# Packed attention and a channel mixer on one core: the value loads by every second partition instead of by head

## The chip, the cores and the metric

The kernel runs on one core of a Trainium2 chip. The metric is the device time of one launch in microseconds (us). A profiled execution also gives a span, the time from the first to the last instruction, and the launch takes a little longer than that. Engines are named as the profile names them: PE (TensorE, the matrix engine), DVE (VectorE), ACT (ScalarE), POOL (GpSimd) and SP (SyncE, which here only issues transfers). A transfer is issued by one instruction of SP and is then carried out by the core's 16 DMA engines.

## The reference

There are 8 batches and 8 heads of 64 elements, with 576 tokens. Each head has 32 pack queries `p`. Everything is float32, except that the mixer's weights are float64 and arrive as pairs of 32-bit words.

```python
scale = 1.0 / np.sqrt(q.shape[-1])
def sm_attn(qq, kk, vv):
    s = scale * np.matmul(qq, kk.transpose(0, 1, 3, 2))
    s = s - np.max(s, axis=-1, keepdims=True)
    a = np.exp(s)
    a = a / (np.sum(a, axis=-1, keepdims=True) + 1e-09)
    return np.matmul(a, vv)
p_packed = sm_attn(p, k, v)          # 32 packed rows per head
attn = sm_attn(q, p_packed, p_packed)
x = attn.transpose(0, 2, 1, 3).reshape(B, S, H * D)
h = x.transpose(0, 2, 1) @ U @ V     # mixing over the 576 tokens, rank 32
u = x + h.transpose(0, 2, 1)
out = u + np.maximum(u @ w_ch1, 0.0) @ w_ch2   # 512 -> 2048 -> 512
```

## The kernel before

**Two stages.** The first stage computes the packed rows `p_packed` of all batches. Its unit of work is one batch and one group `g` of four heads, so there are 16 units (`UN`, line 386). The second stage runs over the 8 batches and does the attention of `q` to the packed rows, the mixing, and the two large matrix products; these are written in three-product form to keep float32 accuracy (`mm3`, line 84).

**The first stage, lines 485 to 536.** In iteration `i` of the loop over units the program turns back the exponentials of unit `i-1`, computes the scores of unit `i`, loads the values of unit `i+1` (`a_load_v`, line 403), transposes the keys of unit `i+1` (`a_turn`), loads the keys of unit `i+2` (`a_load`; with them, once per batch, the pack queries `pn`), and takes the softmax of unit `i`. Then it converts one chunk of the float64 weight `w1` (`some_w1`; the chunk comes by line 137 into a tile `bits`, ACT takes its absolute value at line 143, DVE does lines 78 to 81). After that it multiplies unit `i-2`'s exponentials by its values (`a_pack`, PE line 467, ACT line 469) and transposes the packed rows of unit `i-3` (`a_heads`, ACT line 478). After each second unit `a_heads` writes the tile `ppTa` to device memory by line 483; that tile has one buffer, so the next copy of line 478 waits until the store has been read out. Iterations 4 and later also carry three steps each of the second stage's attention for batch 0 (its queries come by line 206). Iteration 14 starts on the second weight (`load_w2`, line 151; conversion lines 77 to 81 and 158).

**The values.** Token `n` of 576 is written as `n = 9*i + c`, with 64 rows `i` and 9 columns `c`. A unit's values sit in the tile `vt` of 128 partitions by 5 by 256 elements, with three buffers. Columns 0 to 7 of row `i` lie in partitions `2*i` (columns 0 to 3) and `2*i+1` (columns 4 to 7): each head has four columns of 64 elements, 1 KB, in each partition. Column 8 of all heads lies in `vt[:64, 4]` and comes by a transfer of its own (line 410). In `a_pack` every head's part of `vt` is the moving operand of 4 x 4 matmuls of line 467, and line 410's part that of four more; `a_pack` is the only reader.

**What sets the order.** Up to line 547 the order of instructions on every engine, SP included, is set by a planner that simulates the program as it is emitted (`schedule_with_timeline_sim=True`, line 746): it can place an instruction before or after others that the source lists in another order, and it decides which SP position each transfer gets. From line 548 on (`tc.manual_schedule()`) the order is that of the source. SP is one queue: an issue that has to wait holds up all those behind it. All transfers of this kernel go through it.

Of the kernel before, what the change touches and what calls it, by code (L numbers as in the profile page):

```python
# [19 lines left out]
def packed_attention_mixer_kernel(  # L20
# [27 lines left out]
    nc = tc.nc  # L48
    B, H, S, D = q.shape
# [6 lines left out]
    NT = 9  # L56
# [346 lines left out]
    def a_load_v(u):  # L403
        b, g = UN[u]
        vt = ua[u]["v"] = sT.tile([P, 5, 4 * D], F32, name="vt", bufs=3)
        rows = v[b, 4 * g:4 * g + 4].rearrange("h (i c) d -> i c h d", c=NT)
        main = v[b, 4 * g:4 * g + 4].rearrange("h (i c) d -> h i (c d)", c=NT)[:, :, :8 * D]
        for h in range(4):
            nc.sync.dma_start(out=vt[:, h], in_=main[h].rearrange("i (a x) -> i a x", a=2))
        nc.sync.dma_start(out=vt[:64, 4].rearrange("p (h d) -> p h d", h=4), in_=rows[:, 8])  # L410

    def a_p(b):
# [72 lines left out]
    a_load(0)  # L485
    a_load(1)
    a_load_v(0)
    for n in range(4):
        load_w1(n)
# [12 lines left out]
    for i in range(NU):  # L502
# [3 lines left out]
        if i + 1 < NU:  # L506
            a_load_v(i + 1)
            a_turn(i + 1)
# [242 lines left out]
```

## Time and profile before

Three runs took 861.79, 865.04 and 865.39 us; the median is 865.04 us. The profiled execution:

| what | value |
|---|---|
| the profiled execution's own time | 864.15 us |
| its span | 862.1 us |
| PE busy | 822.1 us, 95% of the span |
| DVE busy | 386.2 us, 45% |
| ACT busy | 326.9 us, 38% |
| transfers of `vt` by line 409 | 64 of 128 KB |
| transfers of `vt` by line 410 | 16 of 64 KB |
| last `vt` issue of line 410 | at 119.1 us |

The page gives busy shares for the whole span, but the two stages have different limits, so it is read by stage. Its strips cut the span into 40 slices of 21.6 us; a digit is the busy share in tenths. The chain of waits follows the work that ended last backwards, from each instruction to what released it; an entry such as "DMA bits" spans from a transfer's issue to its landing, and "SPq L409" is time in which the issue of line 409 itself stood in the way. In the timeline a row gives start, length, engine, line, tiles, and in brackets how long the engine was idle before it and what ended that.

### The profile page before, as it was taken

How to read it: one execution, taken by the hardware profiler on the slowest of the kernel's cores; microseconds unless marked ns; L12 is line 12 of the kernel's file. 1: busy time of each engine (PE TensorE's matmuls, PEld its weight loads, DVE VectorE, ACT ScalarE, POOL GpSimd, SP SyncE). 2: the span in 40 equal slices, each digit the busy share in tenths (PEclk: the TensorE clock that was granted, in tenths of full speed). 3: DMA queues.
4: the chain of work that ended last, by engine and by line, in shares of the span. 5: the costliest groups of instructions: out<-in, count | busy, mean ns of one | idle time of the engine just before them, and what ended most of it. 6: DMA issues, size and time to landing. Idle time of an engine off the chain costs nothing.

```text
span 862.1 us, 14613 instructions
## 1 busy us (share of the span) xinstructions
PE 822.1 (95%) x5792; PEld 658.5 (76%) x5792; DVE 386.2 (45%) x935; ACT 326.9 (38%) x1012; POOL 78.5 (9%) x113
## 2 busy tenths in 40 slices
PE   5878779999999999999999999999999999999997
PEld 3545457778888888887878878888888887888886
DVE  5769756896334423433343433334334234342221
ACT  4547655554333432234233332334233332342221
POOL 0002210111010101110111000110011001000000
PEclk9969899999999999999999999999999999999999
DMA  8999942322100110011001100011001100010001
GB/s 282 278 309 305 297 129 81 105 98 86 50 2 3 59 62 1 1 62 49 1 1 62 49 13 1 1 62 50 1 1 62 61 2 1 1 49 1 1 1 61
DMA packets 38979, 59.08 MB, mean 69 GB/s; under 512 B 11776, under 2 KB 21888, under 8 KB 38912
## 3 DMA queue, kind: packets, MB, share of 16 engines
q1 hardware_dynamic: 38912, 58.16, 20.8%
q8 instruction: 45, 0.74, 0.4%
q14 instruction: 22, 0.18, 0.1%
HBM read 47.79 MB, written 10.35 MB: 67 GB/s over the span
## 4 chain that ended last, share of the span: by engine, by line
PE 81%; DMA 7%; DVE 7%; ACT 2%; SPq 2%; issue 1%; POOL 0%; ACTq 0%; POOLq 0%
PE o L86 16%; PE o L88 16%; PE o L87 16%; PE h_ps L86 8%; PE h_ps L88 7%; PE h_ps L87 7%; DMA bits<-in_moe_w_ch_dram 4%; PE t_ps L367 3%; PE t_ps L239 2%; DMA vt<-in_v_dram 2%; PE t_ps L219 1%; DVE os L80 1%; DMA ppTd<-ppTa 1%; PE t_ps L315 1%; DVE os L79 1%
## 5 line engine op out<-in xcount | busy, mean ns | idle before, releaser
L86 PE MATMUL o<-w2h,hh 128*128 128x512 f32 x512 | 207.2, 405 | 0.0
L88 PE MATMUL o<-w2h,hl 128*128 128x512 f32 x512 | 202.8, 396 | 0.0
L87 PE MATMUL o<-w2l,hh 128*128 128x512 f32 x512 | 202.6, 396 | 0.0
L603 DVE SCALAR_TENSOR_TENSOR hl<-h_ps,hh 128x256 fp32r<-128x256 f32 x256 | 103.8, 422 | 204.0 <-ACT hj L602 192.0
L600 ACT ACTIVATE hh<-h_ps 128x256 fp32r<-128x256 f32 x256 | 98.8, 388 | 186.4 <-PE h_ps L88 185.9
L86 PE MATMUL h_ps<-ah,wth 128*128 128x320 f32 (+1 forms) x512 | 157.5, 308 | 2.1 <-DVE hl L603 2.1
L87 PE MATMUL h_ps<-al,wth 128*128 128x320 f32 (+1 forms) x512 | 151.9, 297 | 0.0
L88 PE MATMUL h_ps<-ah,wtl 128*128 128x320 f32 (+1 forms) x512 | 151.8, 296 | 0.0
L86 PEld LDWEIGHTS h_ps<-ah,wth 128*128 128x128 f32 x512 | 97.0, 189 | 33.6 <-issue 25.2
L88 PEld LDWEIGHTS o<-w2h,hl 128*128 128x128 f32 x512 | 96.7, 189 | 23.0
L86 PEld LDWEIGHTS o<-w2h,hh 128*128 128x128 f32 x512 | 97.1, 190 | 21.5 <-issue 4.6
L87 PEld LDWEIGHTS o<-w2l,hh 128*128 128x128 f32 x512 | 97.1, 190 | 16.8
L87 PEld LDWEIGHTS h_ps<-al,wth 128*128 128x128 f32 x512 | 97.2, 190 | 1.9
L88 PEld LDWEIGHTS h_ps<-ah,wtl 128*128 128x128 f32 x512 | 97.3, 190 | 0.0
L374 DVE TENSOR_TENSOR wtl<-t_ps,wth 128x256 fp32r<-128x256 f32 x128 | 48.5, 419 | 93.0 <-ACT wth L373 89.7
L373 ACT CAST wth<-t_ps 128x256 fp32r<-128x256 f32 x128 | 43.3, 374 | 109.9 <-PE t_ps L367 96.5
L330 POOL TENSOR_TENSOR al<-aT,ah 128x320 fp32r<-128x320 f32 (+1 forms) x32 | 26.0, 813 | 210.5 <-ACT ah L329 210.5
L278 POOL TENSOR_TENSOR e<-e,m 128x576 f32<-128x576 f32 x16 | 18.9, 1181 | 257.5 <-DVE m L277 252.7
L367 PE MATMUL t_ps<-w1t,ppT 64*32 64x512 f32 x512 | 36.0, 601 | 0.5 <-ACT ppTa L478 0.5
L226 ACT COPY xT<-t_ps 128x256 f32<-128x256 f32 x60 | 20.3, 392 | 42.1 <-PE t_ps L219 41.3
L329 ACT CAST ah<-aT 128x320 fp32r<-128x320 f32 (+1 forms) x32 | 13.9, 434 | 44.5 <-DVE aT L328 44.5
L219 PE MATMUL k_ps<-ident,kx 128*128 128x128 f32 x128 | 25.3, 344 | 5.6 <-DMA kx<-in_k_dram 2.9
(130 smaller groups left out, 962.3 us busy)
## 6 DMA issues: line engine op xcount, KB each, us to landing
bits<-in_moe_w_ch_dram SPq DMA_DIRECT2D x32, 512.0 KB, 5.4
kx<-in_k_dram SPq DMA_DIRECT2D x16, 576.0 KB, 5.8
x<-in_q_dram SPq DMA_DIRECT2D x16, 576.0 KB, 4.8
vt<-in_v_dram SPq DMA_DIRECT2D x64, 128.0 KB, 4.9
out_dram<-bits SPq DMA_DIRECT2D x32, 256.0 KB, 2.4
pn<-in_p_dram SPq DMA_DIRECT2D x16, 64.0 KB, 5.0
vt<-in_v_dram SPq DMA_DIRECT2D x16, 64.0 KB, 4.5
out_dram<-os SPq DMA_DIRECT2D x8, 128.0 KB, 2.3
```

The costliest lines, as they stand in the source:

```text
L86: nc.tensor.matmul(ps, lhsT=lh, rhs=rh, start=start, stop=False)
L87: nc.tensor.matmul(ps, lhsT=lh, rhs=rl, start=False, stop=False)
L88: nc.tensor.matmul(ps, lhsT=ll, rhs=rh, start=False, stop=stop)
L219: nc.tensor.transpose(t_ps[:, o:o + P], x[:, h, P * j:P * j + P], ident)
L226: nc.scalar.copy(dst, src[:, a])
L278: nc.gpsimd.tensor_tensor(e, e, m.unsqueeze(2).to_broadcast([P, S // 32, 32]), op=ALU.subtract)
L330: nc.gpsimd.tensor_tensor(al[:, g, ns], aT[:, ns], ah[:, g, ns].bitcast(F32), op=ALU.subtract)
L367: nc.tensor.matmul(f_ps[g][xs], lhsT=ppT[b][zs, g, xs], rhs=w1t[h // 2][zs, QW * c:QW * c + QW], start=True, stop=True)
L373: nc.scalar.copy(hi[:, g], f_ps[g][:, cs])
L374: nc.vector.tensor_tensor(lo[:, g], f_ps[g][:, cs], hi[:, g].bitcast(F32), op=ALU.subtract)
L600: nc.scalar.activation(hh[:, ms], src, AF.Relu)
L603: nc.vector.scalar_tensor_tensor(hl[:, ms], src, 0.0, hh[:, ms].bitcast(F32), op0=ALU.max, op1=ALU.subtract)
```

## The change

For each unit, the four transfers that each brought one head to all 128 partitions become two transfers that each bring all four heads to every second partition: the first to partitions 0, 2, ..., 126 (columns 0 to 3), the second to partitions 1, 3, ..., 127 (columns 4 to 7). The bytes, the places where they come from and where they lie in `vt`, and the 1 KB runs stay the same. The transfer of column 8 and everything else in the source stay as they are.

```diff
@@ -404,9 +404,10 @@
         b, g = UN[u]
         vt = ua[u]["v"] = sT.tile([P, 5, 4 * D], F32, name="vt", bufs=3)
         rows = v[b, 4 * g:4 * g + 4].rearrange("h (i c) d -> i c h d", c=NT)
-        main = v[b, 4 * g:4 * g + 4].rearrange("h (i c) d -> h i (c d)", c=NT)[:, :, :8 * D]
-        for h in range(4):
-            nc.sync.dma_start(out=vt[:, h], in_=main[h].rearrange("i (a x) -> i a x", a=2))
+        main = v[b, 4 * g:4 * g + 4].rearrange("h (i c) d -> i h (c d)", c=NT)
+        for a in range(2):
+            nc.sync.dma_start(out=vt[:, :4].rearrange("(i a) h x -> a i h x", a=2)[a],
+                              in_=main[:, :, 4 * D * a:4 * D * a + 4 * D])
         nc.sync.dma_start(out=vt[:64, 4].rearrange("p (h d) -> p h d", h=4), in_=rows[:, 8])
 
     def a_p(b):
```

## The prediction

> **What bounds the kernel now.** I read the strips of the page first, because all of the changed transfers lie in the first stage, and then the groups of issues.
>
> ```profile
> span 862.1 us, 14613 instructions
> ...
> PE   5878779999999999999999999999999999999997
> ...
> DMA  8999942322100110011001100011001100010001
> ...
> vt<-in_v_dram SPq DMA_DIRECT2D x64, 128.0 KB, 4.9
> ...
> vt<-in_v_dram SPq DMA_DIRECT2D x16, 64.0 KB, 4.5
> x<-in_moe_V_dram SPq DMA_DIRECT2D x4, 144.0 KB, 7.8
> ```
>
> From the seventh slice on PE is full and the transfers nearly idle; in the first five slices it is the other way round. The busy time by stretch gives this in numbers; its last two columns are the busy share of the 16 DMA engines and their rate.
>
> ```profile
> core 0: us, PE busy (x) PEld busy (x) DVE busy (x) ACT busy (x) POOL busy (x), PEclk, DMA share, GB/s
> 4.00:112.00 108.00, 83.60 (x1043) 53.11 (x1050) 80.42 (x198) 62.45 (x185) 13.88 (x22) 0.87 0.96 303
> 112.00:122.00 10.00, 7.92 (x148) 4.48 (x132) 3.66 (x10) 5.25 (x17) 3.34 (x10) 1.00 0.51 143
> 122.00:862.00 740.00, 730.07 (x4608) 600.63 (x4608) 302.11 (x727) 257.89 (x810) 60.27 (x73) 1.00 0.10 33
> ```
>
> After 122 us PE is busy for 730 of 740 us: nothing that the change touches is left there, and whatever it gives or takes is a shift of that stage's start. Between 4 and 112 us no compute engine is full (PE has 83.6 of 108 us), but the DMA engines are, at 0.96. So this stretch is limited by bytes per time and by the moments when SP supplies too little. The share that is free, 0.04 of 108 us, is 4.3 us, and no faster issuing can take out more than that there. Between 112 and 122 us the transfers are at half load: there it is latency that counts.
>
> Next the issues themselves, in SP's timeline (start, length, line, how many in a row) around the end of the stage:
>
> ```profile
> 91.17 0.41 SPq L151 DMA_DIRECT2D bits<-in_moe_w_ch_dram  x1
> 91.67 3.15 SPq L409 DMA_DIRECT2D vt<-in_v_dram  x4
> 94.86 0.62 SPq L410 DMA_DIRECT2D vt<-in_v_dram  x1
> 95.58 0.55 SPq L206 DMA_DIRECT2D kx<-in_k_dram  x1
> 96.23 2.49 SPq L409 DMA_DIRECT2D vt<-in_v_dram  x4
> 98.77 0.62 SPq L410 DMA_DIRECT2D vt<-in_v_dram  x1
> ...
> 116.11 2.96 SPq L409 DMA_DIRECT2D vt<-in_v_dram  x4
> 119.12 0.62 SPq L410 DMA_DIRECT2D vt<-in_v_dram  x1
> ```
>
> and the chain of waits, in order of time, at the places where it passes through SP or through a transfer behind these issues:
>
> ```profile
> 54.93 5.47 DMA bits<-in_moe_w_ch_dram
> ...
> 91.17 5.71 DMA bits<-in_moe_w_ch_dram
> 96.89 0.53 SPq L409
> ...
> 99.50 5.25 DMA bits<-in_moe_w_ch_dram
> ...
> 119.84 2.13 DMA ppTd<-ppTa
> ...
> 122.61 0.27 ACT hh L600
> ```
>
> Two things are to be seen. One unit's values hold SP for five issues, 3.15 + 0.62 us here. And the second `vt` issue of the next unit, at 96.89, follows the landing of `bits` at 91.17 + 5.71 = 96.88 us: counted from that `bits` it is the ninth (one, four, one, one, then the first of four, then this one). So an issue waits until the transfer eight before it has landed. Five of those eight places go to one unit's values now.
>
> **The change part by part.** What one issue costs is in the rows of the tile `vt` (shortest, median, longest in ns):
>
> ```profile
> L409 SPq DMA_DIRECT2D vt<-in_v_dram x64: 534/603/1419, 2.8 to 118.5; - x64
> L410 SPq DMA_DIRECT2D vt<-in_v_dram x16: 623/624/1474, 5.4 to 119.1; - x16
> ```
>
> *Removed:* 64 issues of line 409 at 603 ns, 38.6 us of SP. *Added:* 32 issues of a form that the trace lacks: 64 rows by four heads by 1 KB, to every second partition. The nearest row is line 410, which also walks 64 rows by four heads of the same tensor (256-byte runs) at 624 ns; line 409 has 64 rows by two runs. Bounds: 534 ns from below (line 409's shortest), 2 x 603 ns from above, if an issue costs by its number of runs, which doubles. Line 410 has as many runs as the new form and costs 624 ns, so I take that: 32 x 0.624 = 20.0 us. SP saves 18.6 us in all, 1.16 us for each unit (1.34 and 0 at the bounds). The places of the eight that a unit takes fall from five to three.
>
> *Data movement:* the runs stay 1 KB, their number is the same. With nothing else changed the DMA time is the same: I take zero, and put the lower bound also at zero, since neither runs nor bytes get fewer. The upper bound is the slower rival below, from the loads of V.
>
> Most of the 18.6 us lies behind full DMA engines and moves nothing. Three places can move; each needs what the engines did there.
>
> ```profile
> 60.42 0.66 ACT L143 ACTIVATE os<-bits 128x512 f32<-128x512 f32 x1 [1.15 <-DMA bits<-in_moe_w_ch_dram]
> ...
> 104.77 0.67 ACT L77 ACTIVATE os<-bits 128x512 f32<-128x512 f32 x1 [0.35 <-DMA bits<-in_moe_w_ch_dram]
> ...
> 117.81 0.27 ACT L478 COPY ppTa<-t_ps 128x128 f32<-128x128 f32 x1
> ...
> 122.07 0.27 ACT L478 COPY ppTa<-t_ps 128x128 f32<-128x128 f32 x1 [1.83 <-DMA ppTd<-ppTa]
> ```
>
> ```profile
> 120.43 0.31 PE L88 MATMUL h_ps<-ah,wtl 128*128 128x320 f32 x1
> ...
> 123.50 0.41 PE L86 MATMUL h_ps<-ah,wth 128*128 128x320 f32 x1 [2.05 <-DVE hl L603]
> ```
>
> (1) *The end of the stage.* The store of `ppTa` was ready at 117.81 + 0.27 = 118.08 us but is issued at 119.84, right behind the last unit's five value issues. Three issues from 116.11 end at 116.11 + 3 x 0.624 + 0.1 = 118.1 us, so the store goes out 1.7 us earlier. ACT's next `ppTa` copy waits for it (1.83 us), the first `hh` copy is queued behind that on ACT, and PE waits 2.05 us for what follows. The first `h_ps` is complete by 120.43 + 0.31 = 120.74; with `hh` 1.7 us earlier (120.9 instead of 122.61) it is there. I take 1.6 us, off PE's 2.05 us; the rest of the gap, the time of `hh` and `hl` themselves, stays. (2) *The weight chunk issued at 99.50.* With three issues for each unit it is itself the ninth after the `bits` of 91.17 and can go at 96.9, 2.6 us earlier. But ACT waited only 0.35 us for it, being at other work before: 0.35 us. (3) *The chunk issued at 54.93*, behind four issues of line 409. ACT waited 1.15 us for it at 60.42. The stretch just before has free DMA time:
>
> ```profile
> 12.00:14.00 2.00, 0.75 (x4) 0.26 (x2) 1.97 (x4) 0.81 (x2) 0.00 (x0) 1.00 1.02 410
> 32.00:36.00 4.00, 4.00 (x100) 2.49 (x100) 3.83 (x14) 2.71 (x7) 0.24 (x1) 1.00 0.98 193
> ...
> 50.00:54.00 4.00, 2.27 (x15) 1.53 (x15) 3.70 (x10) 2.53 (x8) 0.00 (x0) 1.00 0.69 170
> ```
>
> At 0.69 that is 1.2 us free in 50 to 54 us, so between 0 and 1.15 us can go; the next full stretch may take it back, so I take the middle, 0.6 us. Sum: 1.6 + 0.35 + 0.6 = 2.5 us. The profiled execution took 864.15 us, 2.05 more than its span; 864.15 - 2.5 = 861.6. The median of the three runs is 0.9 us above that execution, so **862.5 us** on the median's scale.
>
> Above the 1.6 us the whole free DMA time, 4.3 us, is the bound: 5.9 us, 859.1 on that scale.
>
> **The rivals.** *Hidden anyway.* The planner sees other transfers and may give SP and the engines another order; then the store at 119.84 may stand behind something else, and the full DMA engines hold the rest: 865.0. For it: 0.96 busy. Against it: the store behind PE's 2.05 us gap was ready 1.7 us before SP issued it.
>
> *More than the sum.* If the eight places are what leaves the DMA engines empty, all 4.3 us go, with the 1.6: 859.1. For it: the wait at 96.89. Against it: the engines have work while SP waits for a landing.
>
> *Slower: engines that write in each other's way.* In 32 to 36 us the DMA engines are full (0.98) at 193 GB/s, where 12 to 14 us shows 410 GB/s at 1.02. In flight then are, for the most part, the four loads of V, each to 32 partitions, with the longest median landing of the page, 7.8 us:
>
> ```profile
> 27.61 2.72 SPq L178 DMA_DIRECT2D x<-in_moe_V_dram  x4
> ```
>
> So a transfer to a part of the partitions can halve the rate although its runs are long. The new form writes 64 partitions at a time. If it too ran at 193 GB/s, the 64 x 128 KB = 8.39 MB would take 43.5 us instead of 27.7 us at the stretch's mean of 303 GB/s: 15.8 us more, 13.8 of them for the 14 units that load before 112 us. The free 4.3 us absorb some: 9.5 us slower, 864.15 + 9.5 + 0.9 = 874.6. It decides as soon as the values' rate falls below 303 x 24.2 / 28.5 = 257 GB/s, where 14 units' 24.2 us grow by 4.3. Against it: these 64 partitions are spread over the whole range, while V's 32 are neighbours, and the two halves follow each other. The trace does not say which engine writes which partition, so I give it a fifth.
>
> The Trainium skill has a rule on this (page "SBUF — State Buffer", section "Door 1: The DMA port swizzle"): a transfer's rate goes by how many of 16 ports its partitions reach, and partitions 0 to 63 reach only eight, 196 GB/s against 328 GB/s for all 128 at 1 MiB. The trace's 193 GB/s for V agrees with it. Taken as a rule on 64 partitions it would price the values at 8.39 MB/196 - 8.39 MB/328 = 17 us more, as an estimate; but by the same section's map every second partition reaches all 16 ports, and then the sum is unchanged. The page says nothing about two engines that meet at one port within a transfer.
>
> *The planner's order alone.* A reorder can also open a gap like the 2.05 us on PE or the 1.15 us on ACT anew; one or two such are 2 to 4 us to either side, which widens all cases.
>
> **How the numbers follow.** Forecast (some 1 to 4 us gained) 0.37; hidden 0.2; more 0.2; slower by the DMA rate or by a worse order 0.23. A measurement of this kernel tells about 0.5%, 4.3 us, from no change: faster means below 860.7, slower above 869.3. Faster: the 0.2 of the larger gain, and 0.1 of the forecast's upper side: 0.3. Slower: 0.23 less what stays under 869.3 of it: 0.21. Same: 0.49. The range reaches from 857 (the bound of 859.1, and 2 us of a lucky order) to 872 (most of the way to 874.6); outside lie some 0.08 on either side. The forecast's own range is 860 to 865.
>
> **What the profile of the changed kernel will show.** The step on SP is right if 32 issues of line 409's place last near 0.62 us; wrong above 0.9. The data step is right if the DMA share in 4 to 112 us stays near 0.96 or falls while the rate is 300 GB/s or more; a rate well under 303 at a share of 1.0 is the slower rival. The end step is right if the last store of `ppTa` follows its copy within 0.3 us and PE's gap ahead of the second `h_ps` falls from 2.05 to about 0.4 us. What would make the prediction wrong is PE's full stage starting more than 4 us from where it does now.

## The result and the profile after

The changed kernel takes 856.45 us (median of 6 runs, 855.9 to 857.36) against 864.18 us for the kernel before beside it (6 runs); the ratio is 0.9904, with a 95% interval of 0.9885 to 0.9924. It is faster by 7.7 us. The forecast was 2.5 us and its range went down to 857 us, so the sign came out as forecast and the gain three times as large. Of the runs below, one execution of e1 (1983.97 us) and one of e4 (1570.26 us, the profiled one) were disturbed; the ratios leave them out, the two medians do not.

The clock that the chip grants to PE does not make this gain: in the runs beside e1 and e9 the kernel before took 863.3 to 864.5 us at its highest mean clocks (0.988 to 0.990), and the changed kernel took 855.9 us at its lowest (0.979).

The page of the changed kernel, its span, two strips and the value transfers:

```profile
span 854.2 us, 14592 instructions
...
PE   5887889999999999999999999999999999999997
...
DMA  9999922332001100011001100011001100010001
...
vt<-in_v_dram SPq DMA_DIRECT2D x32, 256.0 KB, 6.4
...
vt<-in_v_dram SPq DMA_DIRECT2D x16, 64.0 KB, 6.1
```

The first five slices of the DMA strip are now full, and PE's full stretch begins about a third of a slice earlier. Busy time by stretch, the changed kernel first and then the kernel before over the same work (the columns are those of the prediction's table; the last two are the DMA engines' share and GB/s):

```profile
4.00:114.00 110.00, 89.09 (x1182) 56.72 (x1182) 83.43 (x208) 68.78 (x202) 17.04 (x33) 0.91 0.99 311
114.00:854.00 740.00, 729.98 (x4608) 600.72 (x4608) 302.12 (x727) 257.91 (x809) 60.09 (x72) 1.00 0.10 33
```

```profile
4.00:122.00 118.00, 91.53 (x1183) 57.59 (x1182) 84.08 (x208) 67.70 (x201) 17.22 (x32) 0.88 0.92 290
```

The second stage has the same length in both, 740 us with 730 us of PE (the prediction shows the row of the kernel before); it starts 8 us earlier, and that is the whole gain. The first stage moves the same bytes, 110 us x 311 GB/s = 34.2 MB and 118 us x 290 GB/s = 34.2 MB, but the DMA engines stand free for 0.08 x 118 = 9.4 us of it before and for 0.01 x 110 = 1.1 us after. The 8.3 us between make up the gain, within the rounding of the shares.

What one issue costs, by the rows of the tile `vt` (shortest, median, longest in ns):

```profile
L409 SPq DMA_DIRECT2D vt<-in_v_dram x32: 601/617/1483, 2.8 to 109.8; - x32
L411 SPq DMA_DIRECT2D vt<-in_v_dram x16: 611/612/769, 4.4 to 111.2; - x16
```

The new form costs 617 ns, 14 more than the old one (603), though it brings twice the bytes in twice the runs. The lengths of all of SP's issues that start before 112 us, taken one by one, add up to 78.3 us in the kernel before and 63.9 us in the changed one: SP was issuing for 70% of that time and is for 57% now. The rows of a timeline must not be added up for this: a row that merges several issues also spans the waits between them.

The end of the stage, in SP's timeline, then in ACT's and PE's:

```profile
109.19 2.01 SPq L409 DMA_DIRECT2D vt<-in_v_dram  x2
111.25 0.62 SPq L411 DMA_DIRECT2D vt<-in_v_dram  x1
111.96 10.46 SPq L484 DMA_DIRECT2D ppTd<-ppTa  x2
```

```profile
109.52 0.26 ACT L479 COPY ppTa<-t_ps 128x128 f32<-128x128 f32 x1
...
114.61 0.27 ACT L479 COPY ppTa<-t_ps 128x128 f32<-128x128 f32 x1 [1.53 <-DMA ppTd<-ppTa]
```

```profile
115.79 0.41 PE L86 MATMUL h_ps<-ah,wth 128*128 128x320 f32 x1 [2.32 <-DVE hl L604]
```

Here nothing was gained: the store of `ppTa` still stands behind the last unit's values, is issued 111.96 - 109.78 = 2.2 us after its copy ended (109.52 + 0.26), and PE's gap is 2.32 us instead of 2.05.

### The profile page after: what moved, and what is told of

It is laid out like the page before. It is cut to its first block, busy times and chain, and to the rows that moved or that the text cites. A ratio compares the mean times of both kernels' runs of the same rounds, so it can differ in the third digit from the quotient of the medians.

```text
span 854.2 us, 14592 instructions
## 1 busy us (share of the span) xinstructions
PE 819.7 (96%) x5792; PEld 657.7 (77%) x5792; DVE 385.6 (45%) x935; ACT 328.0 (38%) x1012; POOL 78.1 (9%) x113
## 4 chain that ended last, share of the span: by engine, by line
PE 85%; DVE 7%; DMA 4%; ACT 2%; issue 1%; SPq 1%; POOL 0%; POOLq 0%; DVEq 0%; ACTq 0%
PE o L86 16%; PE o L88 16%; PE o L87 16%; PE h_ps L86 8%; PE h_ps L88 7%; PE h_ps L87 7%; PE t_ps L367 4%; DMA bits<-in_moe_w_ch_dram 2%; PE t_ps L219 1%; PE t_ps L239 1%; DVE os L80 1%; PE t_ps L315 1%; PE k_ps L219 1%; PE t_ps L245 1%; DVE os L78 1%
## 5 line engine op out<-in xcount | busy, mean ns | idle before, releaser
L289 POOL TENSOR_TENSOR e<-e,s 128x576 f32<-128x576 f32 x16 | 18.8, 1177 | 114.6 <-DVE s L288 107.9
```

The source lines that it names most:

```text
L289: nc.gpsimd.tensor_tensor(e, e, s.unsqueeze(2).to_broadcast([P, S // 32, 32]), op=ALU.mult)
```

## The experiments

The theories to tell apart were: (A) the number of issues, through SP's time or the eight places that the prediction read from the trace; (B) the every-second-partition form, which might move data better; (C) the planner's new order, which comes with every change in the number of transfers. All ratios are to the kernel before, run beside each. The diffs show only the lines that change: those of e1, e2, e3, e5, e8, e10 and e12 start from the changed kernel, those of e4, e6, e7, e9 and e11 from the kernel before.

**e1: the new form, the old number.**

```diff
-        for a in range(2):
-            nc.sync.dma_start(out=vt[:, :4].rearrange("(i a) h x -> a i h x", a=2)[a],
-                              in_=main[:, :, 4 * D * a:4 * D * a + 4 * D])
+        for a in range(2):
+            for y in range(2):
+                nc.sync.dma_start(out=vt[:, 2 * y:2 * y + 2].rearrange("(i a) h x -> a i h x", a=2)[a],
+                                  in_=main[:, 2 * y:2 * y + 2, 4 * D * a:4 * D * a + 4 * D])
```

> Four transfers for a unit, as before, but each to every second partition and two heads (plus that of column 8). The planner gives every engine, SP too, the order of the kernel before. If the number of issues made the gain (theory A: SP's time and the eight places), this takes as long as before, 863 to 865.5 us. If the planner's new order made it (theory C), the same. If writing every second partition makes the data move better (theory B), 856 to 858 us.

Measured: 864.2 us, ratio 1.0005 (0.999 to 1.0021). The form alone does nothing, for better or worse.

```profile
4.00:122.00 118.00, 90.60 (x1177) 57.82 (x1177) 83.90 (x208) 67.86 (x201) 15.90 (x31) 0.90 0.91 289
```

The same 118 us at 0.91 and 289 GB/s as before. So theory B is out, and so is the rival of engines that write in each other's way. A and C both allow this result.

**e2: three transfers.** The even partitions in one transfer, the odd ones in two of two heads each.

```diff
-        for a in range(2):
-            nc.sync.dma_start(out=vt[:, :4].rearrange("(i a) h x -> a i h x", a=2)[a],
-                              in_=main[:, :, 4 * D * a:4 * D * a + 4 * D])
+        for a, hs in ((0, slice(0, 4)), (1, slice(0, 2)), (1, slice(2, 4))):
+            nc.sync.dma_start(out=vt[:, hs].rearrange("(i a) h x -> a i h x", a=2)[a],
+                              in_=main[:, hs, 4 * D * a:4 * D * a + 4 * D])
```

> Three transfers for a unit: one for the even partitions with four heads, two for the odd with two heads each (plus column 8). Theory A: about half of the gain, 858.5 to 862 us. Theory B: all of it, 856 to 858 us. Theory C: the planner gives an order that is neither that of before nor that of after, so anything from 855 to 867 us.

Measured: 860.56 us, ratio 0.9946 (0.9929 to 0.9964): half of the gain, as A has it.

**e3: two transfers and two small ones.**

```diff
+        for y in range(2):
+            spare = dram.tile([16, D], F32, name=f"spare{u}{y}", tag=f"spare{u}_{y}")
+            nc.sync.dma_start(out=spare, in_=p[b, 4 * g + y, :16])
```

> The changed kernel with two small transfers more for each unit, 4 KB each from device memory to device memory, read by nobody: five issues again, hardly any bytes. Theory A: most of the gain is lost, 860 to 864.5 us (864 if the eight places decide, nearer 860 if SP's time does, since these issues should cost SP less than 0.6 us each). Theory B: 856 to 858 us. Theory C: anything from 855 to 867 us.

Measured: 864.45 us, ratio 0.9998 (0.9984 to 1.0012). Two transfers of 4 KB take the whole gain away. Their issues were not cheap:

```profile
L413 SPq DMA_DIRECT2D spare<-in_p_dram x32: 488/571/1079, 4.2 to 81.0; - x32
```

At 571 ns each they give SP back all the time saved (80.1 us of issuing before 112 us, by the table below), so this run speaks for the issues and not the bytes, but does not say which of SP's time and the places.

**e4 and e9: two of the four heads issued by POOL.**

```diff
-            nc.sync.dma_start(out=vt[:, h], in_=main[h].rearrange("i (a x) -> i a x", a=2))
+            (nc.sync if h < 2 else nc.gpsimd).dma_start(out=vt[:, h], in_=main[h].rearrange("i (a x) -> i a x", a=2))
```

> The transfers of before, one for each head to all partitions, but two of the four are issued by POOL instead of SP, so SP has three issues for a unit as in the changed kernel. Theory A: 855 to 859 us, if POOL's own issuing costs nobody. Theory B: 863 to 866 us. Theory C: anything from 855 to 867 us.

> The kernel with two of the four heads issued by POOL once more (850.6 us against 864.5), for a trace of it: SP has three issues for a unit as in the changed kernel, but this was 6 us faster than the changed kernel. If POOL's queue only frees SP, the stretch from 4 to 112 us should look as in the changed kernel (313 GB/s); if a second queue keeps the DMA engines better filled, the rate there is above 320 GB/s. Time 849 to 853 us.

Measured: 850.59 us, ratio 0.9838 (0.9817 to 0.9858), and again 852.72 us, ratio 0.9869 (0.985 to 0.9888). This is more than the 855 to 859 us that e4's expectation gave theory A. The trace shown is that of e9. With the old form and the old number of transfers, moving issues from SP to POOL gains as much as the change and 4 to 6 us more. It takes time off SP, and, as e6 will show, it adds places too. The rate over the stretch is not what makes the surplus; e9 and then the changed kernel:

```profile
4.00:112.00 108.00, 85.63 (x1178) 53.57 (x1178) 83.15 (x208) 67.97 (x202) 34.55 (x62) 0.94 1.01 314
```

```profile
4.00:112.00 108.00, 87.61 (x1172) 55.45 (x1173) 83.43 (x208) 67.70 (x200) 16.02 (x30) 0.91 0.99 313
```

314 against 313 GB/s: a second queue does not fill the engines better. The end of the stage differs, in PE's timeline of e9:

```profile
113.25 0.41 PE L86 MATMUL h_ps<-ah,wth 128*128 128x320 f32 x1 [0.33 <-DVE hl L603]
```

PE's gap ahead of the second `h_ps` is 0.33 us where the changed kernel has 2.32. That is the place of the prediction's first term: in e9 the store of `ppTa` is issued at 103.43 us, 0.03 us after its copy (103.13 + 0.27), and no copy waits for it. It makes 2.0 of the 3.5 us between the spans of these two traces (850.7 and 854.2); the rest was not traced to a cause.

**e5: two transfers and two cheap small ones.**

```diff
+        for y in range(2):
+            spare = dram.tile([16, P], F32, name=f"spare{u}{y}", tag=f"spare{u}_{y}")
+            nc.sync.dma_start(out=spare, in_=ident[:16])
```

> The changed kernel with two small stores more for each unit (16 rows of 512 bytes to device memory, read by nobody), of a plain form whose issue should cost SP about 0.33 us instead of about 0.6. So five of the eight places for a unit, as before, but SP's time for a unit is about 2.5 us instead of 3.0. If the places decide: 863.5 to 865.5 us. If SP's issue time decides: 859.5 to 862 us (0.66 of the 1.16 us saved are given back, as with three transfers, 860.6).

Measured: 863.1 us against 865.79, ratio 0.9962 (0.9947 to 0.9977): faster by 2.7 us by the medians and 3.3 by the ratio. The kernel before was slower in these runs than the expectation assumed; on the scale of the first runs (864.45 us) the ratio gives 861.2 us, inside the range for SP's time and outside the one for the places. But the added issues were dearer than meant and bunched:

```profile
L413 SPq DMA_DIRECT2D spare<-ident x32: 302/418/1459, 4.2 to 76.7; - x32
```

The last of the 32 is issued at 76.7 us, so the later units ran with three issues. The small transfers of e3 were bunched in nearly the same way (the last at 81.0 us), and e3 kept nothing of the gain. The two kernels differ in what an issue costs, 80.1 against 75.1 us of issuing, so the pair favours a part for SP's time; it does not settle it.

**e6: two of the four heads issued by ACT.**

```diff
-            nc.sync.dma_start(out=vt[:, h], in_=main[h].rearrange("i (a x) -> i a x", a=2))
+            (nc.sync if h < 2 else nc.scalar).dma_start(out=vt[:, h], in_=main[h].rearrange("i (a x) -> i a x", a=2))
```

> The transfers of before, but two of the four heads are issued by ACT, so that the unit keeps five issues and five places (if ACT's transfers share the eight), while SP issues three for each unit. If SP's time decides: 855 to 860 us, worse only by ACT's 19 us of issuing and its waits for a place. If the places decide: 864 us or slower.

Measured: 869.71 us, ratio 1.0047 (1.0032 to 1.0061), slower. By its expectation this is the side of the places. What the eight places are can be read from the records of the issues. Each transfer reports its landing on a semaphore, a counter; the transfers of SP use eight semaphores in turn, and an issue waits for the transfer that last used its own one. In the kernel before none of 212 issues starts before the eighth one ahead of it has landed, while 71 of 213 start before the seventh has. In e6 the transfers issued by ACT use the same eight, so five places for a unit remain, with less issuing on SP (55.2 us before 112 us). In e4 and e9 those issued by POOL have eight others.

But e6 does not show that the places decide. The waits of ACT in the first 125 us (total, times, longest) give a second reason for its loss:

```profile
ACT os L143 <- DMA bits<-in_moe_w_ch_dram: 9.5, 5, 5.1
...
ACT ah L329 <- DMA vt<-in_v_dram: 4.7, 1, 4.7
```

In the kernel before the first of these was 5.5 us, the longest 1.3, and the second is not among ACT's nine longest there. ACT has work of its own in its queue, and that now stands behind issues and their waits.

**e7 and e8: another order, with four and with two transfers.** Both kernels with one move in the source:

```diff
+        if i + 2 < NU:
+            a_load(i + 2)
         if i + 1 < NU:
             a_load_v(i + 1)
             a_turn(i + 1)
-        if i + 2 < NU:
-            a_load(i + 2)
         a_softmax(i)
```

> The kernel before with one move in the source: the keys of unit i+2 are loaded ahead of the values of unit i+1. The planner then gives every engine another order; transfers and work are the same. Theory A (number of issues): within 2 us of 864.3. If order alone is worth as much as the change (theory C): anything from 856 to 872 us.

> The changed kernel with the same move in the source (keys of unit i+2 ahead of the values of unit i+1), another order again. Theory A: 5.5 to 10 us below the kernel with four transfers and this move. Theory C: the difference of the two is anything, also of the other sign.

Measured: 864.59 us, ratio 0.999 (0.9972 to 1.0008), with four; 855.51 us, ratio 0.9883 (0.9865 to 0.9901), with two. The gain of two transfers over four is 9.1 us in this order and was 7.7 us in the first. Theory C is out for the bulk of it. The eight kernels with all issues on SP, by the sum of the lengths of SP's single issues before 112 us:

| kernel | issues for a unit | SP issuing, us | ratio to before |
|---|---|---|---|
| e3 | 5, two of them small | 80.1 | 0.9998 |
| before | 5 | 78.3 | 1 |
| e1 | 5 | 78.3 | 1.0005 |
| e7 | 5 | 77.5 | 0.999 |
| e5 | 5, two of them small | 75.1 | 0.9962 |
| e2 | 4 | 71.9 | 0.9946 |
| e8 | 3 | 64.3 | 0.9883 |
| after | 3 | 63.9 | 0.9904 |

The time follows SP's issuing, but apart from e5 it follows the number of issues as well. The kernels with another queue do not keep to this order: e9 with 64.6 us on SP is at 0.9869, e6 with 55.2 at 1.0047, and e11, below, with 33.8 at 0.997. So SP's time is not the whole account.

**e10, e11, e12: still more by POOL.** The parity transfers by POOL and column 8 by SP (e10); the old four and column 8 by POOL (e11); the parity transfers and column 8 by POOL (e12). Each replaces `nc.sync` by `nc.gpsimd` in the lines concerned; the first of them in e10 and e12:

```diff
-            nc.sync.dma_start(out=vt[:, :4].rearrange("(i a) h x -> a i h x", a=2)[a],
+            nc.gpsimd.dma_start(out=vt[:, :4].rearrange("(i a) h x -> a i h x", a=2)[a],
```

> The changed kernel with both value transfers issued by POOL; SP keeps only that of column 8, one issue for a unit. If SP's issue time still limits the changed kernel: below 852 us, at or under the 850.6 us of two heads by POOL. If the changed kernel is held by the DMA engines alone: 855 to 858 us.

> The four transfers of the kernel before and that of column 8, all issued by POOL; none is left on SP. If SP's time decides, the number of issues no longer matters: 848 to 853 us, as with two. If the number of transfers itself costs the DMA engines: 5 us or more above the kernel with two transfers by POOL.

> The changed kernel with all three transfers of a unit issued by POOL. Against the four-transfer kernel with all by POOL: the same within 2 us if the change acts through SP's time alone; 4 us or more faster if fewer transfers are better for another reason (the DMA engines, the landing).

Measured: 853.47 us, ratio 0.9877 (0.9861 to 0.9893), for e10; 861.71 us, ratio 0.997 (0.9955 to 0.9984), for e11; 853.57 us, ratio 0.9882 (0.9866 to 0.9898), for e12. e10 falls between its two expectations (below 852, 855 to 858), so it leaves open whether SP's time still limits the changed kernel. e11 missed the range for SP's time by 9 us and met the other one, 5 us or more above the kernel with two transfers by POOL: SP issues no values at all, and yet most of the gain is gone. e12 is 8.1 us faster than e11, with no values on SP in either; its expectation took 4 us or more as the sign of a reason other than SP's time. e11's stretch from 4 to 112 us, where POOL is the fifth busy time, and PE's longest wait late in the stage:

```profile
4.00:112.00 108.00, 84.05 (x978) 53.68 (x978) 78.69 (x195) 61.10 (x176) 52.66 (x90) 0.81 0.92 303
```

```profile
98.42 1.54 PE L245 MATMUL t_ps<-ident,aT 128*128 128x128 f32 x6 [4.93 <-DVE aT L293]
```

The DMA engines are free again (0.92), POOL is at 52.7 of 108 us, and PE waits 4.93 us for `aT`. In the chain of waits `aT` stands on DVE behind a weight chunk that took 6.14 us from its issue to its landing:

```profile
88.06 6.14 DMA bits<-in_moe_w_ch_dram
...
97.60 0.78 DVE aT L293
```

So in e11 compute is late. Three causes were not told apart: the planner's order, POOL's five issues for a unit (in e12, with three, POOL is busy for 43.6 us of that stretch), and PE's clock, which is 0.81 in the row above, 0.92 in e12's and 0.91 in the changed kernel's. The clock has a share: over its twelve runs e11 goes from 864.7 us at a mean clock of 0.975 to 857.8 us at 0.991, where e12 took 853.0 and 853.6 us. The lowest median is e4's; e9, the same kernel, is not clear of e10 and e12.

## Why the prediction was wrong

**What bounds the kernel.** Right: the second stage only moved, 740 us in both, and the first stage was held by the DMA engines and by moments of too little supply. The prediction's own sign of being wrong came true: PE's full stage starts 8 us earlier, where more than 4 was to refute it.

**The cost on SP.** Right: 617 ns measured for the issue that was priced at 624, and the runs of 1 KB were as good to every second partition as before (e1).

**The free DMA time: the step that failed.** The prediction let SP's saving work only through three places on the chain, and put the bound of the rest at 4.3 us, the free 0.04 of 4 to 112 us. The stretch from 112 to 122 us it set aside as one where latency counts. At a load of 0.51 that stretch holds another 4.9 us of free DMA time. It was not a fixed tail: over 4 to 122 us the free time is 9.4 us, and 8.3 of them went. So the term "the rest" was sized at nothing in the forecast and at less than half in its bound, while the largest term of the forecast, the end of the stage, gave nothing. That the sign came out right owes nothing to that term.

Both limits that the change eases show in the trace of the kernel before, over the whole stage and not only where the chain of waits names them. From 62 to 70 us SP issues little, because each issue waits for the eighth ahead of it to land. When `bits` is issued at 70.36 us, the seven transfers still in flight are the values and pack queries below, of 64 to 128 KB each, and the DMA engines run low (the last two columns in the second view):

```profile
60.46 3.75 SPq L409 DMA_DIRECT2D vt<-in_v_dram  x4
65.18 0.62 SPq L410 DMA_DIRECT2D vt<-in_v_dram  x1
66.51 2.48 SPq L399 DMA_DIRECT2D pn<-in_p_dram  x2
70.36 0.34 SPq L137 DMA_DIRECT2D bits<-in_moe_w_ch_dram  x1
```

```profile
70.00:72.00 2.00, 1.46 (x13) 1.03 (x11) 2.00 (x8) 2.00 (x8) 0.61 (x2) 1.00 0.55 94
88.00:92.00 4.00, 3.88 (x76) 2.59 (x73) 3.87 (x8) 1.90 (x5) 0.67 (x1) 1.00 0.80 202
```

From 86.34 to 100.5 us SP issues one transfer after another with at most 0.12 us between them, and the engines are at only 0.80 in 88 to 92 us: there SP is not held up, and its issuing is too slow. A third part is neither: before the last unit's values SP waits 1.6 us, until 116.1 us, for PE to release a buffer of `vt` (line 467).

**The three places.** (1) The end of the stage, 1.6 us, did not come: the last unit's issues still stood ahead of the store and took 2.01 + 0.62 us instead of 1.87, while the copy was ready sooner after their start (0.6 us against 2.0). PE's gap is 2.32 us. That the place is real is shown by e9, where the store goes out at once and the gap is 0.33 us. (2) and (3) cannot be followed one by one, since the planner's order changed everywhere; whatever they gave is within the 8.3 us.

**The rivals.** "More than the sum" was the nearest: it named the empty DMA engines, but its price, 859.1, carries the same cut at 112 us and the end term that did not come. Its mechanism, the eight places, is neither shown to be the whole of it nor refuted: e5 beside e3 speaks for a part of SP's time, e6 and e12 beside e11 for something other than it. "Hidden anyway" is refuted by the result. The slower rival is refuted by e1; with the page "SBUF — State Buffer" of the Trainium skill, section "Door 1: The DMA port swizzle", the trace agrees as far as its map goes: every second partition cost no rate (289 against 290 GB/s), while 193 GB/s was the rate with V's loads to 32 neighbouring ones in flight. The planner's order alone was worth 1 to 2 us in e7 and e8, by ratios whose intervals do not exclude zero.

**Open:** how much of the gain is SP's time and how much the eight places (e3 alone cannot say, beside e5 it leans to SP's time; e6 leans to the places but brought a cost of its own; e4 and e9 ease both), what made the rest of e9's surplus, and the cause of e11's loss. That fewer and larger transfers make the gain is shown; which of the two limits they ease more is not.

## What to carry to other kernels

Add up the issue times of a queue, one issue at a time, as one would the busy time of an engine, although the page does not count them, and see how many transfers the program can have in flight. Here SP issued for 70% of the first 112 us, with at most eight transfers in flight, and the DMA engines were free for 9.4 us, though the chain of waits went through SP only at a few places; no run shows from what share on issuing costs time. There, fewer and larger transfers for the same bytes were worth time, and so was another engine's queue, if that engine had little else in it and places of its own (two heads by POOL gained, by ACT lost). And take free DMA time over the whole stage, its thin tail too, when it is used as a bound.

## What was not expected of the hardware

What an issue costs SP does not go by its bytes: 571 ns for the 4 KB of e3's small transfers, 617 ns for the 256 KB of the new form, 328 ns (median) for the 512 KB of a weight chunk by line 151. So a transfer of 4 KB that nobody reads was nearly as dear here as half of a unit's values. Transfers issued by POOL on a queue of its own ran beside SP's without raising the rate when the engines were full (314 against 313 GB/s).
